# Attention before two expert layers: the multiplication of x and its high part's copy queued behind the score of 128 keys

## The chip, the cores and the metric

The kernel runs on one core of a Trainium2 chip. The metric is the device time of one execution in microseconds; the median of three executions is 2105.64 us. TensorE does the matrix products, VectorE (DVE) and ScalarE (ACT) the elementwise work and the reading of the accumulators, GpSimd (POOL) elementwise work on on-chip data, and SyncE (SP) issues the DMAs.

## The reference, cut to what matters

```python
# attention: q, k, v of (4 batches, 8 heads, 576 positions, 64)
scores = scale * np.matmul(q, k.transpose(0, 1, 3, 2))
scores = np.where(block_i >= block_j, scores, -1e9)      # blocks of 64 positions
scores = scores - np.max(scores, axis=-1, keepdims=True)
attn = np.exp(scores)
attn = attn / (np.sum(attn, axis=-1, keepdims=True) + 1e-09)
x = np.matmul(attn, v)       # then turned to (2304 tokens, 512)
# first layer
h = x @ w_in
x = np.maximum(0.01 * h, h) @ w_out
# second layer: a gate over 8 experts, balanced by 8 rounds of row and column sums
...
for e in range(E):
    out += P[:, e:e + 1] * (np.maximum(x @ w1[e], 0.0) @ w2[e])
```

A query block of 64 positions sees the key blocks up to its own. The x that the attention gives is what the first layer multiplies.

## The kernel before, in words

The attention comes first. Its 32 heads are taken in pairs: NP = 16 pairs, and a pair's two heads share the 128 partitions. Query block i (0 to 8) of a pair needs 64 * (i + 1) keys, so its score is a product of 64, 128, ... 512 columns; the ninth block has 576 keys and is done as two products of 288. Three accumulator banks (tag "sc") go round among the scores, so the score of a block takes the bank that the exponential three scores earlier has read.

For each block `score(p, i)` issues, in this order: the product (line 323, tile `sc`); on VectorE the maximum over the keys, negated (line 324, tile `nmax`); on ScalarE the exponential, with its sum (line 332, tile `ex`). The exponentials are then turned on TensorE 128 columns at a time, four turned tiles to a bank (`turn_attn`, line 363, tile `tr`) and copied out by ScalarE or VectorE (lines 370 and 372, tile `at`). `weigh` multiplies them with the values (lines 385 and 388, tile `av`, one buffer of two banks).

`split_x(p)` ends a pair. On VectorE one multiplication takes the accumulators of the values by the reciprocal sums (line 396, `xs`, in which `by_feature` holds the reciprocals, spread by DMA). On ScalarE a copy rounds the result to the high part of x (line 405, `xhfirst` or `xhlate`), and on GpSimd a subtraction gives the low part (line 406). Where a batch crosses the border between the two x tiles, copy and subtraction are each cut in two.

The work of the pairs is staggered. In pass p of the loop the scores of pair p + 1 are taken in the order 8, 7, 0, 6, 1, 5, 2, 4, 3, and beside each score stands work of other pairs: the queries and keys of pair p + 2 are turned (`turn_q`, `turn_k`, `turn_tail`) and those of pair p + 3 loaded, the exponentials of pair p are turned, and the values of pair p - 1 are weighed and its x split. Beside score 7 stood, before, the turn of the keys, the value products, `split_x` of pair p - 1 and the first turn of pair p:

```python
7: [("fol", turn_k), ("far", load_rows, kraw, k), *values, ("prv", split_x), ("cur", turn_attn, 0)],
...
1: [],
```

TensorE's instructions run in the order of this text (`tc.manual_schedule` names it alone). The order of the other engines is set by a planner, which reorders by its own reckoning of when each instruction's inputs are ready. `tc.issue_after(t)` adds an edge: instructions traced inside the block that run on the engine of `t` are planned behind `t`. It is used for two things before: the steps that split the first layer's weights (two behind score 8, three behind score 7) are queued behind the latest maximum, and the spreading of the sums behind the latest load of values.

The first layer (its products stand at lines 499 and 519) follows directly on TensorE, then the experts, which take most of the span; neither holds a changed line.

Of the kernel before, what the change touches and what calls it, by code (L numbers as in the profile page):

```python
# [27 lines left out]
def f32(ap):  # L28
    return ap.bitcast(F32)
# [7 lines left out]
def block_attention_mlp_moe(  # L37
# [15 lines left out]
    nc = tc.nc  # L53
# [39 lines left out]
    def x_parts(c, t0, t1):  # L93

        if t0 < XCUT:
            return [t[:, c, t0:t1] for t in x_first]
        return [t[:, c, t0 - XCUT:t1 - XCUT] for t in x_late]
# [117 lines left out]
    def attention(att, ps_sc, ps_tr, ps_av):  # L215
        qraw = att.tile([P, NFULL, P], F32, name="qraw")
        kraw = att.tile([P, NFULL, P], F32, name="kraw")
# [93 lines left out]

        latest = [None]

        def score(p, i):
            n = BLK * (i + 1)
            cuts = [(0, n)] if n <= 512 else [(0, n // 2), (n // 2, n)]
            nm, sm = nmax[p % 2], ssum[p % 2]
            part = []  # L320
            for s, (lo, hi) in enumerate(cuts):
                sc = ps_sc.tile([P, 512], F32, name="sc", tag="sc")[:, 0:hi - lo]
                nc.tensor.matmul(sc, qbd[p % 2][:, i, :], kT[p % 2][:, lo:hi], start=True, stop=True)  # L323
                latest[0] = nc.vector.tensor_reduce(  # L324
                    out=nm[:, i + s:i + s + 1], in_=sc, axis=AX.X, op=ALU.max, negate=True
                )
                part.append(sc)
            x = nm[:, i:i + 1]
            if len(cuts) > 1:
                nc.vector.tensor_tensor(out=x, in0=x, in1=nm[:, i + 1:i + 2], op=ALU.min)  # L330
            for s, (lo, hi) in enumerate(cuts):
                nc.scalar.activation(  # L332
                    out=ex[p % 2][:, off[i] + lo:off[i] + hi], in_=part[s], func=AF.Exp,
                    bias=x, scale=1.0, accum_out=sm[:, i + s:i + s + 1],
                )
            if len(cuts) > 1:
                nc.gpsimd.tensor_tensor(
                    out=sm[:, i:i + 1], in0=sm[:, i:i + 1], in1=sm[:, i + 1:i + 2], op=ALU.add
                )
# [51 lines left out]
                )  # L391

        def split_x(p):
            b, hp = divmod(p, NPAIR)
            t = av.pop(p)
            nc.vector.tensor_tensor(  # L396
                out=xs.rearrange("p (i q) -> p i q", q=BLK), in0=t[:, o:o + S].rearrange("p (i q) -> p i q", q=BLK),
                in1=by_feature[p % 2].rearrange("p (q i) -> p i q", i=NQ), op=ALU.mult,
            )
            t0, t1 = b * S, (b + 1) * S  # L400
            cuts = [t0, XCUT, t1] if t0 < XCUT < t1 else [t0, t1]
            for u0, u1 in zip(cuts, cuts[1:]):
                hi, lo = x_parts(hp, u0, u1)
                y = xs[:, u0 - t0:u1 - t0]
                nc.scalar.copy(out=hi, in_=y)
                nc.gpsimd.tensor_tensor(out=lo, in0=y, in1=f32(hi), op=ALU.subtract)

        NP = B * NPAIR
# [4 lines left out]
        values = [("prv", weigh, 0, h, part) for part in range(2) for h in range(2)]  # L413
        values += [("prv", weigh, c, h, 1) for c in range(1, NKC) for h in range(2)]
        beside = {
            8: [("fol", turn_q), ("far", load_rows, qraw, q)],
            7: [("fol", turn_k), ("far", load_rows, kraw, k), *values, ("prv", split_x), ("cur", turn_attn, 0)],
            0: [("cur", turn_attn, 1)],
            6: [("cur", turn_attn, 2), ("nxt", load_v)],
            1: [],  # L420
            5: [("fol", turn_tail), *tails_far],
            2: [("cur", turn_attn, 3)],
            4: [("cur", turn_attn, 4), ("cur", spread_totals)],
# [33 lines left out]
        for p in range(-1, NP + 1):  # L457
            who = {"prv": p - 1, "cur": p, "nxt": p + 1, "fol": p + 2, "far": p + 3}
            if 0 <= p < NP:
                totals(p)  # L460
            for t, i in enumerate(turn_order if p >= 0 else opening):
                if p + 1 < NP:
                    score(p + 1, i)
                for w, f, *a in (beside if p >= 0 else beside_opening)[i]:
                    if 0 <= who[w] < NP:
                        f(who[w], *a)
                for _ in range({0: 2, 1: 3}.get(t, 0) if p >= 0 else 0):
                    if steps:
                        with ExitStack() as queued:
                            if p + 1 < NP:  # L470
                                queued.enter_context(tc.issue_after(getattr(latest[0], "ins", latest[0])))
                            steps.pop(0)()
# [50 lines left out]
    with (  # L523
        tc.tile_pool(name="att", bufs=1) as att,
        tc.tile_pool(name="ps_sc", bufs=3, space=bass.MemoryType.PSUM) as ps_sc,
        tc.tile_pool(name="ps_tr", bufs=3, space=bass.MemoryType.PSUM) as ps_tr,
        tc.tile_pool(name="ps_av", bufs=1, space=bass.MemoryType.PSUM) as ps_av,
    ):
        with tc.manual_schedule(engines={mybir.EngineType.PE}):
            attention(att, ps_sc, ps_tr, ps_av)  # L530
# [345 lines left out]
    for m, (r, b, f, first, last) in enumerate(todo):  # L876
# [11 lines left out]
        if r + 1 == len(runs):  # L888
            k = f - first
# [68 lines left out]
    for n in range(0, NGR, 2):  # L958
        p, e, i = groups[n]
# [74 lines left out]
```

## Time and profile before

| what | value |
|---|---|
| median of three runs | 2105.64 us (2105.45 to 2106.79) |
| the profiled execution's own time | 2106.03 us |
| its span, first to last instruction | 2104.2 us |
| mean granted TensorE clock | 1.000 |
| TensorE busy | 2095.8 us, 10776 matmuls |
| weight loads busy | 1846.2 us |
| VectorE, ScalarE, GpSimd busy | 1428.0, 898.3, 478.3 us |
| last value product of the attention, start | 204.4 us |
| first product of the first layer, start | 204.57 us |

Busy matmul time counts each matmul from its start to a modelled end; matmuls overlap, so the starts of consecutive groups say more than their durations. An instruction's row can likewise reach a little past the start of the next on the same engine. A wait is put down to the instruction that released it, as far as the trace's semaphore events show it.

### The profile page before, as it was taken

The page shows a single profiled execution, that of the slowest core. Times are in us where ns is not written, and L with a number is a line of the kernel's source. Part 1 is how long each engine was busy: PE and PEld are TensorE (multiplying, and loading weights), DVE is VectorE, ACT ScalarE, POOL GpSimd, SP SyncE. Part 2 cuts the span into 40 slices and gives each one's busy share as a digit, 9 for nine tenths or more (in the row PEclk, how much of TensorE's full clock was granted, in tenths as well). Part 3 has the DMA queues.
Part 4 walks back from the last instruction along what each step waited for, and adds up shares of the span by engine and source line. Part 5 has one row for each costly group of instructions (what it writes and reads, how often), then busy time and mean ns, then how long its engine had stood idle before and what let it go on. Part 6 is the DMA issues. An engine that isn't in the chain of part 4 may idle for free.

```text
span 2104.2 us, 28785 instructions
## 1 busy us (share of the span) xinstructions
PE 2095.8 (100%) x10776; PEld 1846.2 (88%) x10776; DVE 1428.0 (68%) x2321; ACT 898.3 (43%) x1859; POOL 478.3 (23%) x526
## 2 busy tenths in 40 slices
PE   9999999999999999999999999999999999999999
PEld 6666898988899899899899889989989988998998
DVE  7786656565468766766777676676678667667665
ACT  7776332222344443443453444344345344434432
POOL 2222212131003212221222221222122122122210
PEclk9999999999999999999999999999999999999999
DMA  5542111010022212212212221221222222122120
GB/s 139 131 121 75 41 40 51 31 56 25 1 61 81 72 49 81 81 41 80 81 60 91 81 71 51 81 81 41 80 81 82 69 80 72 50 81 81 41 81 30
DMA packets 153533, 142.99 MB, mean 68 GB/s; under 512 B 65073, under 2 KB 122417, under 8 KB 153393
## 3 DMA queue, kind: packets, MB, share of 16 engines
q1 hardware_dynamic: 152192, 140.86, 22.5%
q8 instruction: 84, 1.38, 0.3%
q14 instruction: 57, 0.46, 0.1%
q10 hardware_dynamic: 1200, 0.30, 0.1%
HBM read 136.33 MB, written 4.79 MB: 67 GB/s over the span
## 4 chain that ended last, share of the span: by engine, by line
PE 97%; DVE 1%; DMA 0%; ACT 0%; issue 0%; SPq 0%; DVEq 0%; ACTq 0%
PE o L829 37%; PE h_ps L775 33%; PE h_ps L499 9%; PE o L519 9%; PE sc L323 3%; PE av L388 2%; PE tr L363 1%; DVE xs L396 1%; DVE nmax L324 0%; ACT ex L332 0%; DMA qraw<-in_q_dram 0%; DVE at L372 0%; PE qm L297 0%; PE km L303 0%; PE l_ps L633 0%; PE av L385 0%
## 5 line engine op out<-in xcount | busy, mean ns | idle before, releaser
L829 PE MATMUL o<-w2h,xhlate 128*128 128x512 f32 x1152 | 402.6, 390 | 0.0
L829 PE MATMUL o<-w2h,xllate 128*128 128x512 f32 x1152 | 401.6, 389 | 0.0
L783 ACT COPY s<-h_ps 128x384 f32<-128x384 f32 x288 | 138.0, 480 | 555.1 <-PE h_ps L775 555.0
L792 DVE TENSOR_TENSOR c<-h_ps,s 128x384 f32<-128x384 f32 x288 | 155.8, 554 | 313.1 <-PE h_ps L775 303.2
L716 POOL TENSOR_TENSOR wa<-wraw 128x256 f32<-128x256 f32 x96 | 88.0, 917 | 1170.6 <-DVE w1l L734 1144.3
L775 PE MATMUL h_ps<-xhS,w1h 128*128 128x384 f32 x768 | 257.1, 335 | 0.0
L775 PE MATMUL h_ps<-xlS,w1h 128*128 128x384 f32 x768 | 256.5, 334 | 0.0
L775 PE MATMUL h_ps<-xhS,w1l 128*128 128x384 f32 x768 | 256.5, 334 | 0.0
L829 PEld LDWEIGHTS o<-w2h,xllate 128*128 128x128 f32 x1152 | 216.2, 188 | 45.5
L829 PEld LDWEIGHTS o<-w2h,xhlate 128*128 128x128 f32 x1152 | 216.2, 188 | 43.4
L829 PE MATMUL o<-w2l,xhlate 128*128 128x512 f32 x576 | 224.7, 390 | 0.0
L829 PE MATMUL o<-w2l,xllate 128*128 128x512 f32 x576 | 224.4, 390 | 0.0
L842 DVE SCALAR_TENSOR_TENSOR xa<-o,pr,xa 128x512 f32<-128x512 f32 x264 | 189.2, 741 | 50.1 <-PE o L829 50.1
L775 PE MATMUL h_ps<-xhA,w1l 128*128 128x384 f32 x576 | 193.0, 335 | 0.0
L775 PE MATMUL h_ps<-xhA,w1h 128*128 128x384 f32 x576 | 193.0, 335 | 0.0
L775 PE MATMUL h_ps<-xlA,w1h 128*128 128x384 f32 x576 | 192.7, 335 | 0.0
L734 DVE TENSOR_TENSOR w1l<-wraw,w1h 128x512 fp32r<-128x512 f32 x192 | 172.6, 936 | 1.5 <-ACT w1h L733 1.5
L734 DVE TENSOR_TENSOR w1l<-wa,w1h 128x512 fp32r<-128x512 f32 x192 | 160.4, 838 | 0.2 <-ACT w1h L733 0.2
L798 ACT ACTIVATE xllate<-c 128x384 fp32r<-128x384 f32 x144 | 75.7, 526 | 184.1 <-DVE c L792 184.1
L775 PEld LDWEIGHTS h_ps<-xhS,w1h 128*128 128x128 f32 x768 | 144.2, 188 | 0.1
L775 PEld LDWEIGHTS h_ps<-xlS,w1h 128*128 128x128 f32 x768 | 144.2, 188 | 0.0
L775 PEld LDWEIGHTS h_ps<-xhS,w1l 128*128 128x128 f32 x768 | 144.1, 188 | 0.0
(155 smaller groups left out, 3995.6 us busy)
## 6 DMA issues: line engine op xcount, KB each, us to landing
wraw<-in_moe_w_dram SPq DMA_DIRECT2D x192, 512.0 KB, 4.3
wraw<-in_moe_w_in_dram SPq DMA_DIRECT2D x16, 512.0 KB, 3.7
wraw<-in_moe_w_out_dram SPq DMA_DIRECT2D x16, 512.0 KB, 3.6
by_feature<-row SPq DMA_DIRECT2D x32, 144.0 KB, 3.2
out_dram<-xa SPq DMA_DIRECT2D x18, 256.0 KB, 2.0
qraw<-in_q_dram SPq DMA_DIRECT2D x32, 128.0 KB, 2.8
vraw<-in_v_dram SPq DMA_DIRECT2D x32, 128.0 KB, 2.5
kraw<-in_k_dram SPq DMA_DIRECT2D x30, 128.0 KB, 3.2
```

Source lines behind the costliest of these rows:

```text
L323: nc.tensor.matmul(sc, qbd[p % 2][:, i, :], kT[p % 2][:, lo:hi], start=True, stop=True)
L388: nc.tensor.matmul(av[p][r, 512 + P * max(c - 1, 0):512 + S - P], lhsT, a[:, q0:, :], start=c == 0, stop=c == NKC - 1,)
L499: nc.tensor.matmul(ps[:, 0:n], w[:, c, cols], x, start=c == 0 and s == 0, stop=c == KC - 1 and s == 2,)
L519: nc.tensor.matmul(ps[:, 0:n], w[:, cut], h[:, 0:n], start=start and m == 0, stop=stop and m == 2)
L716: nc.gpsimd.tensor_tensor(out=one[:, 0], in0=a21, in1=a22, op=ALU.add)
L734: nc.vector.tensor_tensor(out=lo, in0=x, in1=f32(hi), op=ALU.subtract)
L775: mm = nc.tensor.matmul(ps, w[:, c], x[:, c], start=first and c == 0 and s == 0, stop=c == 1 and s == 2, skip_group_check=True,)
L783: nc.scalar.copy(out=t, in_=bank[n, name][:, 0:HT])
L792: nc.vector.tensor_tensor(out=c, in0=x, in1=part[n, add], op=ALU.add)
L798: nc.scalar.activation(out=hi, in_=x, func=AF.Relu),
L829: mm = nc.tensor.matmul(o, h, w, start=m == 0, stop=m == 11)
L842: nc.vector.scalar_tensor_tensor(out=a, in0=o, scalar=pr[:, tt, e:e + 1], in1=a, op0=ALU.mult, op1=ALU.add)
```

## The change

`split_x` moves from the work beside score 7 to the work beside score 1 (128 keys), three scores later in the text. Its body becomes `multiply_x`, and `split_x` calls it inside a block that plans its VectorE instruction behind the latest maximum and its ScalarE copies behind the latest exponential; in the order of the passes these are the last ones of score 1 of pair p + 1. The edges exist where pair p + 2, counted from the pair that is multiplied, is still to be scored. The work itself is unchanged.

```diff
-        latest = [None]
+        latest, latest_exp = [None], [None]
...
             for s, (lo, hi) in enumerate(cuts):
-                nc.scalar.activation(
+                latest_exp[0] = nc.scalar.activation(
                     out=ex[p % 2][:, off[i] + lo:off[i] + hi], in_=part[s], func=AF.Exp,
...
         def split_x(p):
+            with ExitStack() as queued:
+                if p + 2 < NP:
+                    for t in (latest[0], latest_exp[0]):
+                        queued.enter_context(tc.issue_after(getattr(t, "ins", t)))
+                multiply_x(p)
+
+        def multiply_x(p):
             b, hp = divmod(p, NPAIR)
             t = av.pop(p)
...
-            7: [("fol", turn_k), ("far", load_rows, kraw, k), *values, ("prv", split_x), ("cur", turn_attn, 0)],
+            7: [("fol", turn_k), ("far", load_rows, kraw, k), *values, ("cur", turn_attn, 0)],
...
-            1: [],
+            1: [("prv", split_x)],
```

## Rows read from the trace of the kernel before

**Rows 1.** Busy time by engine in two passes, from value products to value products.
```profile
core 0: us, PE busy (x) PEld busy (x) DVE busy (x) ACT busy (x) POOL busy (x), PEclk, DMA share, GB/s
52.52:64.69 12.17, 12.11 (x79) 8.37 (x78) 9.20 (x22) 9.20 (x29) 4.13 (x5) 1.00 0.55 142
125.55:137.81 12.26, 12.24 (x80) 8.44 (x79) 10.24 (x25) 9.29 (x30) 1.99 (x4) 1.00 0.43 101
```

**Rows 2.** The chain of waits in the pass from 52.9 us: start, us, what.
```profile
55.52 1.20 DVE xs L396
...
58.87 0.59 PE sc L323 x2
```

**Rows 3.** TensorE in order of time in that pass: start us, us, what.
```profile
56.48 0.92 PE L323 MATMUL sc<-kT,qbd 128*128 128x448 f32 x2
...
58.54 0.27 PE L308 MATMUL qk_tail<-ident,tails 128*128 128x128 f32 x1
58.87 0.59 PE L323 MATMUL sc<-kT,qbd 128*128 128x192 f32 x2
...
59.83 0.81 PE L323 MATMUL sc<-kT,qbd 128*128 128x320 f32 x2
60.48 0.60 PE L363 MATMUL tr<-ident,ex 128*128 128x128 f32 x4
60.91 0.60 PE L323 MATMUL sc<-kT,qbd 128*128 128x256 f32 x2
...
61.89 1.14 PE L323 MATMUL sc<-kT,qbd 128*128 128x288 f32 x4
...
63.30 1.02 PE L323 MATMUL sc<-kT,qbd 128*128 128x512 f32 x2
64.16 0.60 PE L303 MATMUL km<-ident,kraw 128*128 128x128 f32 x4
```

**Rows 4.** VectorE in the same pass; in brackets idle time before, and who ended it.
```profile
55.52 1.20 DVE L396 TENSOR_TENSOR xs<-av,by_feature 128x576 f32<-128x576 f32 x1 [1.89 <-PE av L388]
...
56.76 0.69 DVE L372 COPY at<-tr 128x512 f32<-128x512 f32 x1
57.43 0.62 DVE L324 TENSOR_REDUCE nmax<-sc 128x1 f32<-128x448 f32 x1
57.98 0.68 DVE L372 COPY at<-tr 128x512 f32<-128x512 f32 x1
58.57 0.75 DVE L324 TENSOR_REDUCE nmax<-sc 128x1 f32<-128x128 f32 x2
...
60.68 0.49 DVE L324 TENSOR_REDUCE nmax<-sc 128x1 f32<-128x320 f32 x1 [0.82 <-PE sc L323]
...
62.58 0.94 DVE L324 TENSOR_REDUCE nmax<-sc 128x1 f32<-128x288 f32 x2 [0.20 <-PE sc L323]
```

**Rows 5.** ScalarE in the same pass.
```profile
56.75 0.67 ACT L405 CAST xhfirst<-xs 128x576 fp32r<-128x576 f32 x1
...
58.09 0.63 ACT L332 ACTIVATE ex<-sc,nmax 128x448 f32<-128x448 f32 x1 [0.37 <-DVE nmax L324]
...
59.32 0.37 ACT L332 ACTIVATE ex<-sc,nmax 128x128 f32<-128x128 f32 x1
...
59.68 0.57 ACT L332 ACTIVATE ex<-sc,nmax 128x384 f32<-128x384 f32 x1
...
60.63 0.59 ACT L370 COPY at<-tr 128x512 f32<-128x512 f32 x1
61.20 0.53 ACT L332 ACTIVATE ex<-sc,nmax 128x320 f32<-128x320 f32 x1
...
62.04 0.58 ACT L370 COPY at<-tr 128x512 f32<-128x512 f32 x1 [0.22 <-PE tr L363]
62.52 0.48 ACT L332 ACTIVATE ex<-sc,nmax 128x256 f32<-128x256 f32 x1
...
63.50 1.20 ACT L289 ACTIVATE qbd<-qm 64x512 f32<-64x512 f32 x2 [0.41 <-PE qm L297]
```

## Prediction: what the change does to the time

> **What bounds the kernel now.** I read the page first: TensorE is busy for almost the whole span at the full granted clock, and the attention, where alone the changed lines run, takes the first 204.6 us of 2104.2. There the program is a loop over pairs of heads, so I cut it into single passes, from the first value product of one pass to that of the next. A pass lasts 12.17 us (12.26 us in the four passes where the high part's copy is cut in two), and TensorE is busy in 12.11 us of it, VectorE in 9.20 to 10.24, ScalarE in 9.2 [rows 1]. Busy matmuls overlap, so that alone doesn't say that TensorE sets the pass. The chain of waits comes next, and it seems to speak for the change: behind the value products it leaves TensorE, goes through the multiplication of x on VectorE (1.20 us), and comes back to TensorE only with the score of 192 keys at 58.87 [rows 2]. Last I read one pass in order of time, engine by engine, to see whether that detour holds TensorE up.
>
> It doesn't. The 512-key score takes 0.86 us from its start (63.30) to the next start (64.16), that is 1.68 ns for each key; the second 288-key score therefore starts 0.48 us behind the first. VectorE, idle for 0.20 us before, began the first 288-key maximum at 62.58, 0.69 us behind the start of its score (61.89): 0.48 for the columns and 0.21 until the maximum can begin [rows 3, 4]. By the same sum the 448-key score that starts at 56.48 can be taken up at 56.48 + 0.75 + 0.21 = 57.44, and it was at 57.43 [rows 3, 4]. VectorE could have been there only 0.07 us sooner: from a copy of the turned attention to the next maximum it needs 0.59 us (57.98 to 58.57), and there it took 0.67 (56.76 to 57.43) [rows 4]. So the maximum of 448 keys waits for TensorE's own score, not for the multiplication; the two ways tie, and the chain shows one of them. Behind it come the exponential at 58.09, and the score of 192 keys at 58.87, which takes the bank that this exponential frees [rows 3, 5]. That wait stays when the multiplication goes.
>
> **What the change removes.** Both moved instructions sit in idle time now. VectorE waits 1.89 us for the value products before the multiplication [rows 4]; ScalarE is idle for 0.37 us before the exponential of 448 keys even with the copy ahead of it [rows 5]. I put the removal at nothing in the ten passes of the common kind: the cover is the wait for TensorE's 448-key score. In the four longer passes it may give back their difference, 12.26 - 12.17 = 0.09 us each [rows 1], 0.4 us in all. The bounds: nothing below, 0.09 us in all 14 passes (1.3 us) above.
>
> **What it adds.** The code holds the multiplication behind the maximum of 128 keys on VectorE and the copy behind the exponential of 128 keys on ScalarE, in the 14 passes with a next pair to score and a previous one to multiply (p = 1 to 14; the last two passes have no such edge). No instruction and no DMA is added; SP's queue keeps its order. The POOL subtraction follows the copy by its data, about 3 us later; POOL is busy for 4.13 us of such a pass [rows 1], and I put it at nothing. The accumulators that the multiplication reads are next written at the next pass's value products, some 5 us later; nothing too.
>
> What counts is what now queues behind the two. On VectorE the pair of maxima of 128 and 384 keys starts at 58.57 and takes 0.75 us, of which some 0.55 belong to the 384 keys (between 0.49 for 320 and 0.62 for 448), so the one of 128 hands over at about 58.77 [rows 4]. The multiplication then runs until 59.97, and the maximum of 384 keys until 60.52 instead of 59.32. VectorE gets that back soon: it has 0.82 us of idle time before the 320-key maximum and 0.20 before the next [rows 4]. ScalarE doesn't. From 58.09 to 62.52 it stands still only for 0.22 us [rows 5]. The exponential of 128 keys starts at 59.32 and lets the 320-key score go at 59.83, 0.51 us later; the one of 448 keys needs 0.78 (58.09 to 58.87) [rows 3, 5]. In between I take 0.62, 0.67 and 0.73 us for 256, 320 and 384 keys. In the new order the copy starts with the end of the multiplication at 60.00 and ends at 60.67 (its 0.67 us [rows 5]), and the exponential of 384 keys, at 59.68 now, starts there. Then:
> - The score of 256 keys needs the bank of that of 384: 60.67 + 0.73 = 61.40 in place of 60.91 [rows 3], late by 0.49 us.
> - The exponential of 320 keys follows 1.52 us behind that of 384 (59.68 to 61.20) [rows 5]: 62.19, its bank free at 62.86. The second half of the score of 576 keys needs it: 61.89 + 0.49 + 0.48 = 62.86. No further wait.
> - The copy of turned attention at 62.04 follows 0.62 us behind it when its 0.22 us of idle time goes, and the exponential of 256 keys 0.48 us behind that [rows 5]: 63.29, its bank free at 63.91. The score of 512 keys would start at 63.30 + 0.49 = 63.79 [rows 3], and waits until 63.91: late by 0.61 us in all.
>
> Whole durations are a little long: the 0.59 us copy at 60.63 is followed 0.57 us later, the 0.58 us one at 62.04 after 0.48 us [rows 5]. With 0.58 for the copy the delay is 0.52 us. I take 0.55, nearer to the lower end as the rows mostly overlap. The next pass begins with ScalarE's and VectorE's waits for TensorE, so nothing is carried over and nothing won back. Below, the cost is nothing if the planner finds a gap for the copy (third rival); above, it is the order of the first rival.
>
> The sum: 14 passes by 0.55 us is 7.7 us, less 0.4 us, 7.3 us. The profiled execution took 2106.03 us with a span of 2104.2; it would be 2113.3 with 2111.5. It lies 0.4 us above the median of 2105.64, so against the runs it is 2112.9; I say 2113.0.
>
> The Trainium skill, PSUM — Partial Sum Buffer, section Engine vs sequencer instructions, calls the queues of ScalarE and VectorE strict first in, first out. That speaks against this change: a copy that waits for the multiplication holds up the exponential behind it, and by that rule the 7.3 us stand; if later work could pass it, the cost would be near nothing. No row here shows work passing.
>
> **The rivals.**
> - *A worse order on ScalarE.* The planner, not the text, orders VectorE and ScalarE. The copy of turned attention that stands at 60.63 [rows 5] reads transposes that lie between the scores at 58.87 and 59.83 [rows 3], so it becomes ready at about the moment the multiplication ends. If it goes first (60.00 to 60.57), the high part's copy ends at 61.2, and the 256-key score starts at 61.2 + 0.73 = 61.9, late by nearly 1 us: 14 by 0.95, 13.3 us, 2118.5. For it: a near tie. Against it: it stands later in the text.
> - *The gaps take it in part.* If the planner lets the maxima of 384 and 192 keys go first, the multiplication fills the 0.82 us gap [rows 4], the exponential of 384 keys keeps its time, and only the end of ScalarE's run is late: 0.6 us for the copy, less the 0.22 us gap and the 0.16 us by which the bank of the 256-key score (62.52 + 0.62) is free ahead of the score of 512 keys at 63.30 [rows 3, 5], some 0.2 us a pass: 2.8 us, 2108.4. Against it: the multiplication is ready long before that maximum.
> - *No effect.* ScalarE has 0.41 us of idle time before the scaling of the turned queries at 63.50 [rows 5]. A copy planned behind the exponential of 256 keys would cost nothing: 2105.3.
> - *Faster.* The chain of waits is right and the tie is not one. The score of 192 keys starts 0.33 us behind the start of the tail's transpose (58.54), and one transpose takes 0.11 (four in 0.43 from 60.48) [rows 3]: 0.22 us of waiting. It goes when the 448-key maximum starts sooner by that much: 3.1 us in 14 passes, with the 1.3 us above 4.4, so 2101.2. It decides from the point where that maximum starts earlier than 0.95 us behind its score. Against it: the sum that gave 57.44. The Trainium skill, Perfetto Trace Analysis, section Identifying the Most-Contended Engine, measures TensorE by its weight loads, not by its matmuls. The loads take 8.37 of 12.17 us, 69%, less than VectorE's 76% [rows 1]; by that TensorE has room, and this rival would win. The starts of the scores, spaced by their columns, disagree.
>
> **How the numbers follow.** My forecast 0.45, the worse order 0.17, the gaps 0.18, no effect 0.12, faster 0.05; 0.03 are left for a planner that also changes its orders behind the attention. Within 0.2% (4.2 us, about what these runs can tell from no change) lie the gaps and no effect. So faster 0.05, same 0.30, slower 0.65. The likeliest case alone spans 2111.5 to 2115. The range must reach down to no effect and up to the worse order: 2105.0 to 2119.0.
>
> **What would show it.** Right: passes 1 to 14 of about 12.7 us and the last two unchanged; ScalarE's copy to the high part between the exponentials of 128 and 384 keys, with a wait for the multiplication before it; TensorE's 256-key score waiting for an exponential; the 448-key maximum still 0.95 us behind its score; VectorE idle for some 2.6 us ahead of the 64-key maximum; everything behind the attention only shifted. Wrong: the copy elsewhere in ScalarE's order, passes of 12.2 us or less, or a different order of the matmuls behind 205 us.

## The result, and the profile after

| | before | after |
|---|---|---|
| median of four executions | 2105.6 us (2105.45 to 2106.79) | 2119.84 us (2119.23 to 2120.92) |
| ratio of after to before | | 1.0067, 95% interval 1.0049 to 1.0084 |
| the profiled execution: time, span | 2106.03, 2104.2 us | 2119.23, 2117.4 us |
| a pass of the common kind, a long one | 12.17, 12.26 us | 13.13, 13.22 us |
| first value product of the first pass, first product of the first layer | 28.18, 204.57 us | 27.66, 217.67 us |

The kernel became slower, by 14.2 us in the medians and 13.2 us between the two profiled executions. The first layer starts 13.1 us later and the span behind it has not changed (2117.4 - 217.67 = 1899.7 against 2104.2 - 204.57 = 1899.6), so all of it lies ahead of the first layer, in the attention. The 14 passes with the new edges lost 13.6 us together: twelve of them 0.95 to 0.97 us each, and the two last, which are shorter (11.67 and 9.27 us before), 0.97 and 1.15. The first value product came 0.5 us earlier in this execution. The forecast was 2113.0 us with a range up to 2119.0: the sign was right, the forecast loss about half of the measured one, and the time 0.8 us above the range.

The busy time by engine in a pass of each kind, from value products to value products, as in [rows 1]:

```profile
core 0: us, PE busy (x) PEld busy (x) DVE busy (x) ACT busy (x) POOL busy (x), PEclk, DMA share, GB/s
53.92:67.05 13.13, 12.38 (x80) 8.40 (x79) 9.16 (x22) 9.14 (x28) 4.13 (x5) 1.00 0.54 131
132.71:145.92 13.21, 12.38 (x79) 8.39 (x78) 10.17 (x25) 9.23 (x29) 1.98 (x4) 1.00 0.40 91
```

No work was added: VectorE, ScalarE and GpSimd are busy for as long as before, to within 0.1 us. TensorE's busy time rises from 12.11 to 12.38 us with the same matmuls, since a modelled matmul grows where it waits (the score of 256 keys below: 0.70 us in place of 0.60), and for the other 0.75 us of the pass it stands still. Where, its timeline shows (the pass that starts with the value products at 53.92, so 1.40 us later than the one of [rows 3]):

```profile
57.87 0.92 PE L323 MATMUL sc<-kT,qbd 128*128 128x448 f32 x2
...
60.27 0.59 PE L323 MATMUL sc<-kT,qbd 128*128 128x192 f32 x2
...
61.23 0.81 PE L323 MATMUL sc<-kT,qbd 128*128 128x320 f32 x2
61.87 0.60 PE L363 MATMUL tr<-ident,ex 128*128 128x128 f32 x4
63.17 0.70 PE L323 MATMUL sc<-kT,qbd 128*128 128x256 f32 x2 [0.69 <-ACT ex L332]
...
64.25 1.14 PE L323 MATMUL sc<-kT,qbd 128*128 128x288 f32 x4
...
65.66 1.02 PE L323 MATMUL sc<-kT,qbd 128*128 128x512 f32 x2
```

Up to the transposes at 61.87 every start lies exactly 1.40 us behind that of before, or 1.39 (the scores of 448, 192 and 320 keys: 56.48, 58.87, 59.83). The score of 256 keys, due at 60.91 + 1.40 = 62.31, comes at 63.17: 0.86 us late. From there to the next score it takes 1.08 us in place of 0.98, and from there on nothing more is lost (64.25 to 65.66 is 1.41, as 61.89 to 63.30 was). 0.86 + 0.10 is the 0.96 us of the pass.

VectorE in the same pass, and then ScalarE:

```profile
57.63 0.22 DVE L324 TENSOR_REDUCE nmax<-sc 128x1 f32<-128x64 f32 x1 [2.61 <-PE sc L323]
...
58.83 0.62 DVE L324 TENSOR_REDUCE nmax<-sc 128x1 f32<-128x448 f32 x1
...
59.97 0.28 DVE L324 TENSOR_REDUCE nmax<-sc 128x1 f32<-128x128 f32 x1
60.16 1.18 DVE L403 TENSOR_TENSOR xs<-av,by_feature 128x576 f32<-128x576 f32 x1
61.26 0.55 DVE L324 TENSOR_REDUCE nmax<-sc 128x1 f32<-128x384 f32 x1
```

```profile
59.49 0.64 ACT L332 ACTIVATE ex<-sc,nmax 128x448 f32<-128x448 f32 x1 [1.08 <-DVE nmax L324]
...
60.72 0.37 ACT L332 ACTIVATE ex<-sc,nmax 128x128 f32<-128x128 f32 x1
...
61.38 0.67 ACT L412 CAST xhfirst<-xs 128x576 fp32r<-128x576 f32 x1 [0.20 <-DVE xs L403]
61.96 0.58 ACT L370 COPY at<-tr 128x512 f32<-128x512 f32 x1
62.44 0.58 ACT L332 ACTIVATE ex<-sc,nmax 128x384 f32<-128x384 f32 x1
```

Two things are to be seen. The maximum of 448 keys starts 0.96 us behind its score (57.87 to 58.83; before 0.95), with the multiplication no longer ahead of it: nothing was gained there. And ahead of the exponential of 384 keys now stand three things in a row: the wait for the multiplication, the high part's copy, and the copy of a group of turned exponentials, which before stood behind the exponential of 192 keys, at 60.63 [rows 5]. The planner has moved that copy too, ahead of the exponentials of 384 and 192 keys: below, this is called the swap, and that copy the swapped copy. The 256-key score follows 0.73 us behind the start of the exponential of 384 keys.

### The profile page after: what moved, and what is told of

Its sections match the earlier page's. It is cut to its first block, busy times and chain, and to the rows that moved or that the text cites. A ratio compares the mean times of both kernels' runs of the same rounds, so it can differ in the third digit from the quotient of the medians.

```text
span 2117.4 us, 28785 instructions
## 1 busy us (share of the span) xinstructions
PE 2099.0 (99%) x10776; PEld 1846.3 (87%) x10776; DVE 1426.1 (67%) x2321; ACT 897.7 (42%) x1859; POOL 479.2 (23%) x526
## 4 chain that ended last, share of the span: by engine, by line
PE 95%; DVE 2%; ACT 1%; issue 1%; DMA 1%; POOL 0%; SPq 0%; DVEq 0%; POOLq 0%; ACTq 0%
PE o L836 37%; PE h_ps L782 33%; PE h_ps L506 9%; PE o L526 9%; PE sc L323 2%; PE av L388 2%; PE tr L363 1%; DVE xs L403 1%; DVE nmax L324 1%; ACT ex L332 0%; ACT at L370 0%; DMA wraw<-in_moe_w_in_dram 0%; PE l_ps L640 0%; PE qm L297 0%; PE av L385 0%
```

## The experiments

**The theory** behind the first four (A): the score of 256 keys waits for the bank that the exponential of 384 keys reads, and everything that puts this exponential off counts, also the swapped copy. Against it stood B, VectorE's late maximum alone, and C, the swap of the two ScalarE instructions alone. All ratios are to the kernel before, run beside the experiments on the same chip (its medians there: 2105.76 us for experiments 1 to 4, 2106.27 for 5 to 8, and 2105.64 for 9 and 10, which ran on another chip than the rest).

**1. The swapped copy put back behind the exponential of 192 keys** (`t1_turn_behind`), the rest as changed:

```diff
             if g in ((0, 3, 5) if p + 1 < NP else (0, 2, 4, 6)):
-                nc.scalar.copy(out=dst, in_=tr[:, 0:n])
+                with ExitStack() as queued:
+                    if g == 3 and p + 1 < NP:
+                        queued.enter_context(tc.issue_after(getattr(latest_exp[0], "ins", latest_exp[0])))
+                    nc.scalar.copy(out=dst, in_=tr[:, 0:n])
```

> The changed kernel with one more edge: ScalarE's copy of the fourth group of turned exponentials is planned behind the exponential of 192 keys, as it stood before the change. The high part's copy alone then stands between the exponentials of 128 and 384 keys. Theory A (the 256-key score waits for the bank of the exponential of 384 keys, which the multiplication, the high part's copy and the copy of the turned group hold up one after the other): the exponential of 384 keys starts 0.48 us sooner than in the changed kernel, a pass is late by about 0.5 us in place of 0.95, and the kernel takes 2112.6 us (2111.5 to 2113.5). Theory B (VectorE's late maximum of 384 keys alone): no change, 2119.8. Theory C (the swap of the two ScalarE instructions is the whole loss): 2105.6.

Measured: 2112.73 us, ratio 1.0032 (1.0020 to 1.0045); passes of 12.64 us. ScalarE, and the score that waits:

```profile
60.96 0.67 ACT L415 CAST xhfirst<-xs 128x576 fp32r<-128x576 f32 x1 [0.21 <-DVE xs L406]
61.54 0.58 ACT L332 ACTIVATE ex<-sc,nmax 128x384 f32<-128x384 f32 x1
```

```profile
62.26 0.70 PE L323 MATMUL sc<-kT,qbd 128*128 128x256 f32 x2 [0.21 <-ACT ex L332]
```

This is the order that the prediction had summed, and its time is nearly the one forecast (2113.0), in part by luck: a pass lost 0.47 us where 0.55 were summed, and the 0.4 us that were taken off for the long passes did not come. The swap alone is the other half: 13.13 - 12.64 = 0.49 us a pass.

**2. Only the copy moved** (`t2_copy_edge`): the edge for the multiplication left out, so that the planner puts it where it stood before. The diff is against the changed kernel.

```diff
-                    for t in (latest[0], latest_exp[0]):
+                    for t in (latest_exp[0],):
```

> The changed kernel with the edge for ScalarE's copy alone; the multiplication is planned as early as before the change. Theory A: the copy adds 0.58 us ahead of the exponential of 384 keys; its bank comes free 0.08 us late, and the run of exponentials ends 0.2 us late: 14 passes by 0.2, less 0.4 us: 2108.0 us (2106.5 to 2109.5). Theory B: 2105.6. Theory C: 2105.6.

Measured: 2108.22 us, ratio 1.0011 (1.0002 to 1.0020); passes of 12.33 us, 0.16 above those of before. The time is the one expected, but in other pieces: the 256-key score comes 0.05 us late, its follower 0.11 more, the score of 512 keys does not wait, and the long passes (12.42 us) gave nothing back. ScalarE and TensorE:

```profile
60.49 0.58 ACT L332 ACTIVATE ex<-sc,nmax 128x384 f32<-128x384 f32 x1
```

```profile
61.21 0.70 PE L323 MATMUL sc<-kT,qbd 128*128 128x256 f32 x2
```

**3. The multiplication moved, the copy out of the way** (`t3_mult_alone`): `split_x` cut into its two halves, the copy with the subtraction moved to the end of the run of exponentials, the swapped copy held as in the first experiment.

```diff
-            1: [("prv", split_x)],
+            1: [("prv", mult_x)],
...
-            3: [("cur", turn_attn, 5), ("cur", turn_attn, 6)],
+            3: [("cur", turn_attn, 5), ("cur", turn_attn, 6), ("prv", copy_x)],
```

> The multiplication behind the maximum of 128 keys as in the changed kernel; the high part's copy goes behind the exponential of 256 keys, and the copy of the turned group stays behind the exponential of 192 keys. So ScalarE's order up to there has nothing added, and VectorE's is that of the change. Theory A: the exponential of 384 keys starts with the end of its maximum, some 0.75 us late; its bank is late by 0.26 us, the end of the run by 0.38: 14 by 0.38 is 5.3, 2110.5 us (2109 to 2112). Theory B: 2119.8. Theory C: 2105.6.

Measured: 2111.21 us, ratio 1.0025 (1.0015 to 1.0035); passes of 12.54 us, the long ones now too. ScalarE stands still before the exponential of 384 keys, until VectorE has its maximum; the copy of the turned group, whose transposes stand at 61.97, keeps its place behind:

```profile
63.13 0.58 ACT L332 ACTIVATE ex<-sc,nmax 128x384 f32<-128x384 f32 x1 [0.67 <-DVE nmax L324]
...
64.10 0.58 ACT L373 COPY at<-tr 128x512 f32<-128x512 f32 x1
```

```profile
61.97 0.60 PE L363 MATMUL tr<-ident,ex 128*128 128x128 f32 x4
...
63.85 0.70 PE L323 MATMUL sc<-kT,qbd 128*128 128x256 f32 x2
```

**4. Multiplication early, copy at the end of the run** (`t4_copy_late`): the second experiment with `split_x` beside score 3, which makes the edge one to the exponential of 256 keys.

```diff
-            1: [("prv", split_x)],
+            1: [],
...
-            3: [("cur", turn_attn, 5), ("cur", turn_attn, 6)],
+            3: [("cur", turn_attn, 5), ("cur", turn_attn, 6), ("prv", split_x)],
```

> The multiplication as early as before the change, the high part's copy behind the exponential of 256 keys, in ScalarE's 0.41 us of idle time. The copy no longer precedes the exponential of 64 keys, which makes the four long passes 0.09 us shorter. Theory A: 2105.2 us (2104.5 to 2106). Theory B and C: 2105.6. If the chain of waits through the multiplication counted before the change, nothing moves here either, since the multiplication stays.

Measured: 2107.42 us, ratio 1.0009 (1.0001 to 1.0018): 1.7 us more than before, where no loss was expected. The score of 256 keys no longer waits, and most passes last 12.17 us, two of the four long ones too; but two last 12.84 and 12.92, and three 12.28 to 12.36. GpSimd's and VectorE's timelines ahead of the first of these, from its value products at 88.56 on:

```profile
87.90 1.41 POOL L413 TENSOR_TENSOR xlfirst<-xs,xhfirst 128x576 fp32r<-128x576 f32 x1
```

```profile
87.99 1.34 DVE L330 TENSOR_TENSOR nmax<-nmax 128x1 f32<-128x1 f32 x1
...
92.44 1.20 DVE L403 TENSOR_TENSOR xs<-av,by_feature 128x576 f32<-128x576 f32 x1
...
94.29 0.62 DVE L324 TENSOR_REDUCE nmax<-sc 128x1 f32<-128x448 f32 x1
```

The minimum of the two halves of the ninth block, one column, takes 1.34 us in place of 0.10, and ends with GpSimd's subtraction, which the late copy has moved beside it. VectorE's weight steps then run late, the multiplication starts 3.9 us behind the value products in place of 3.0, and the maximum of 448 keys starts 1.8 us behind its score: here the multiplication holds up TensorE. A held minimum alone does not do it. It takes 1.27 us ahead of passes of 12.17 us too, where at most three weight steps follow and VectorE catches up before the multiplication. Ahead of the pass of 12.92 us, a second instruction is held: a weight step, 0.71 us in the kernel before, beside a GpSimd subtraction of weights of 1.27 us:

```profile
116.10 1.52 DVE L182 SCALAR_TENSOR_TENSOR wraw<-wraw,wb 128x512 f32<-128x512 uint32 x1
```

**What the four say together.** From the start of the exponential of 384 keys to that of the score of 256 keys it takes 0.73 us in the changed kernel and 0.72 in the first three experiments (61.54 to 62.26 and 63.13 to 63.85 in two of them), while in the fourth the exponential starts early and the score comes 1.23 us behind it, as before (59.68 to 60.91). The distance between TensorE's scores of 320 and 256 keys is 1.08 us before, and 1.13, 1.34, 1.46 and 1.94 in these four kernels, while that from the exponential stays. The score's delay is that exponential's. B and C each fail on the first three.

**5 and 6. Four banks for the scores, two for the transposes**, with the kernel before (`t5_before_four`) and with the changed one (`t6_after_four`):

```diff
-        tc.tile_pool(name="ps_sc", bufs=3, space=bass.MemoryType.PSUM) as ps_sc,
-        tc.tile_pool(name="ps_tr", bufs=3, space=bass.MemoryType.PSUM) as ps_tr,
+        tc.tile_pool(name="ps_sc", bufs=4, space=bass.MemoryType.PSUM) as ps_sc,
+        tc.tile_pool(name="ps_tr", bufs=2, space=bass.MemoryType.PSUM) as ps_tr,
```

> The kernel before with four accumulator banks for the scores and two for the transposes, in place of three and three. Theory A (scores wait for the bank of the exponential three scores back): the waits of the scores of 192 and 320 keys, 0.22 and 0.09 us a pass, go; passes of some 11.85 us, 15 of them: 2101.0 us (2099.5 to 2103). Theory D (TensorE's own stream sets the pass, the gaps are not waits for a bank): 2105.6.

> The changed kernel with four banks for the scores and two for the transposes. The score of 256 keys then takes the bank of the 128-key exponential, which stands ahead of the moved copy. Theory A: most of the 14 us of the change go, 2103 us (2101 to 2107), within 0.3% of the kernel before with the same banks. Theory E (ScalarE or VectorE as a whole is too late, whatever bank a score takes): the distance between the two stays 14 us, 2115.

Measured: 2101.40 us for the kernel before with these banks, ratio 0.9975 (0.9966 to 0.9985), passes of 11.78 us: the waits of the scores of 192 and 320 keys were waits for a bank. The 192-key score now follows 0.11 us behind the tail's transpose, in place of 0.33 [rows 3]:

```profile
59.06 0.27 PE L308 MATMUL qk_tail<-ident,tails 128*128 128x128 f32 x1
59.17 0.49 PE L323 MATMUL sc<-kT,qbd 128*128 128x192 f32 x2
```

This version is faster than both kernels. The changed kernel with these banks missed its expectation: 2114.67 us, ratio 1.0039 (1.0025 to 1.0053), 13.3 us behind its counterpart, so the distance stayed. That is the figure of theory E; but no score waits there any more, and the loss is again a wait for one bank. TensorE's wait has gone to the transposes behind the score of 320 keys, and VectorE's timeline shows for what:

```profile
87.08 0.70 PE L323 MATMUL sc<-kT,qbd 128*128 128x320 f32 x2
88.62 0.63 PE L363 MATMUL tr<-ident,ex 128*128 128x128 f32 x4 [0.84 <-DVE kT L292]
```

```profile
86.43 1.18 DVE L403 TENSOR_TENSOR xs<-av,by_feature 128x576 f32<-128x576 f32 x1
87.53 0.81 DVE L324 TENSOR_REDUCE nmax<-sc 128x1 f32<-128x384 f32 x2
88.26 0.21 DVE L292 COPY kT<-qk_tail 128x64 f32<-128x64 f32 x1
```

With two banks these transposes need the one of the tail, and the tail's copy stands behind the multiplication and two maxima.

**7. The multiplication narrowed in the kernel before** (`t7_narrow`), to ask whether its early place cost anything. The kernel leaves out the multiplication of eight of the nine query blocks:

```diff
+        nc.gpsimd.memset(xs, 0.0)
...
             nc.vector.tensor_tensor(
-                out=xs.rearrange("p (i q) -> p i q", q=BLK), in0=t[:, o:o + S].rearrange("p (i q) -> p i q", q=BLK),
-                in1=by_feature[p % 2].rearrange("p (q i) -> p i q", i=NQ), op=ALU.mult,
+                out=xs[:, 0:BLK], in0=t[:, o:o + BLK], in1=by_feature[p % 2][:, 0:BLK], op=ALU.mult,
             )
```

> The kernel before with the multiplication on 64 columns in place of 576; the other columns of its result are zeros, set once at the start. VectorE is free about 1 us sooner for the maxima behind it. Theory A (the maximum of 448 keys waits for TensorE's own score, so the early multiplication is covered): passes of 12.17 us, the four long ones too, 2105.2 us (2104.6 to 2106). Theory F (the chain of waits is right, the multiplication holds up the scores): 0.2 to 0.3 us a pass less, 2101 to 2102.5.

Measured: 2105.78 us against 2106.27, ratio 0.9997 (0.9988 to 1.0006); passes of 12.17 us, the long ones too. TensorE and VectorE:

```profile
56.37 0.92 PE L323 MATMUL sc<-kT,qbd 128*128 128x448 f32 x2
```

```profile
55.41 0.22 DVE L396 TENSOR_TENSOR xs<-av,by_feature 128x64 f32<-128x64 f32 x1 [1.89 <-PE av L388]
...
57.33 0.62 DVE L324 TENSOR_REDUCE nmax<-sc 128x1 f32<-128x448 f32 x1
```

With the multiplication 1 us shorter the maximum of 448 keys still starts 0.96 us behind its score, and the time is the same within the interval. F falls.

**8. GpSimd's subtraction in pieces** (`t8_pieces`), in the kernel of experiment 4:

```diff
-                nc.gpsimd.tensor_tensor(out=lo, in0=y, in1=f32(hi), op=ALU.subtract)
+                for g in range(0, u1 - u0, 192):
+                    cut = slice(g, min(g + 192, u1 - u0))
+                    nc.gpsimd.tensor_tensor(out=lo[:, cut], in0=y[:, cut], in1=f32(hi)[:, cut], op=ALU.subtract)
```

> The kernel with the copy behind the exponential of 256 keys, and GpSimd's subtraction cut into pieces of at most 192 columns. Theory G (the one-column minimum on VectorE, which took 1.27 us in place of 0.10 while the subtraction ran, waits for the GpSimd instruction under way): it takes 0.6 us or less, the passes of 12.8 us go, and the kernel takes 2105.4 us (2104.8 to 2106.5). Otherwise, where the loss has another cause: 2107.4.

Measured: 2107.10 us against 2106.27, ratio 1.0003 (0.9994 to 1.0012). The held minimum takes 0.42 to 0.45 us, where it took up to 1.34, and the passes of 12.8 us are gone; single ones of 12.42 and 12.34 remain. In the pass of 12.42 us the weight step at line 182 is still held (1.48 us), beside a GpSimd subtraction that was not cut. The wait of the minimum is shown; the time missed the range of theory G and lies between the two expectations, and whether it differs from that of experiment 4 the intervals don't say.

**9 and 10. The halves of the change with four and two banks**: the second experiment (`t9_copy_four`) and the third (`t10_mult_four`) with the banks of experiments 5 and 6, and no other edit.

> Four banks for the scores and two for the transposes, with ScalarE's copy of the high part behind the exponential of 128 keys and the multiplication as early as before the change. Theory H (what the moved copy cost with three banks, 0.16 us a pass, was the wait for the bank of the exponential of 384 keys; with four banks no score takes that bank so soon): passes of 11.8 us as in the kernel before with four banks, 2101.4 us (2100 to 2103). Theory E (ScalarE as a whole is too late): 0.2 us a pass more, 2104.5.

> Four banks for the scores and two for the transposes, the multiplication behind the maximum of 128 keys, the copy of the high part at the end of ScalarE's run. Theory H: VectorE alone makes the whole loss with these banks, since the key tail's copy stands behind the multiplication and two maxima, and the transposes that need its bank wait 0.8 us: passes of 12.8 us, 2114.5 us (2113 to 2117). Theory E, with ScalarE as the cause: the 0.67 us of the copy are gone from its run, passes of 12.2 us or less, 2106.

Measured: 2108.34 us for the copy alone, ratio 1.0013 (1.0004 to 1.0022), passes of 12.33 us, and 2117.94 us for the multiplication alone, ratio 1.0058 (1.0045 to 1.0070), passes of 12.94 us. The first lies above what either theory gave: 0.55 us a pass more than the 11.78 of experiment 5. The wait is again one for a bank of the transposes, here for ScalarE's copy of the turned group, which the planner puts behind the moved copy and the exponential of 384 keys:

```profile
76.07 0.76 PE L363 MATMUL tr<-ident,ex 128*128 128x128 f32 x5 [0.46 <-ACT at L370]
```

```profile
74.30 0.66 ACT L412 CAST xhfirst<-xs 128x576 fp32r<-128x576 f32 x1
74.86 0.58 ACT L332 ACTIVATE ex<-sc,nmax 128x384 f32<-128x384 f32 x1
75.43 0.58 ACT L370 COPY at<-tr 128x512 f32<-128x512 f32 x1
```

In the second the transposes behind the 320-key score wait 0.84 us for the tail's copy, as H said; its time is 0.9 us above the range given. No run had more banks in both rings at once, so it is not shown whether the loss would then go.

## Why the prediction was right or wrong

- *What bounds a pass.* Right. TensorE's stream sets it, with waits for banks that experiment 5 found worth 0.39 us a pass, and the early multiplication was covered by the wait for the 448-key score: the changed kernel and the narrowed multiplication both leave that maximum 0.96 us behind its score. The chain of waits in [rows 2] named a path that was only as long as another (0.08 us apart by the rows that the prediction reads, not 0.07).
- *The sign and the place.* Right. The score of 256 keys waits for the bank of the exponential of 384 keys, in all 14 passes, and the last passes and all behind the attention are as before.
- *The copy's place.* The step that failed is the sentence that the copy ends at 60.67 and "the exponential of 384 keys, at 59.68 now, starts there". The planner put the copy of the turned group in between, at a price of 0.49 us a pass. In the pass of [rows 5] that exponential would stand at 61.04 (62.44 - 1.40) and the 256-key score at 61.77 in place of 61.40. The sum took ScalarE's order of before as given, with the one copy put in. With the turned group's copy put back, the kernel takes 2112.73 us.
- *The first rival* had this instruction, the cost of a pass (0.95 us; measured 0.96) and nearly the time (2118.5), but in the other order, turned group first, and 0.17 of the chance. On the chip the high part's copy went first and the turned group's second, ahead of an exponential that was late itself: its maximum ended at 61.81, ScalarE was free of the high part's copy at 61.96. I had weighed the turned group only against the high part's copy, not against the exponential, which the multiplication makes late on VectorE. Why the planner ranks the two so is not shown; that it does is in the rows of ScalarE. The measured time lies above this rival's, and above the range whose upper end it set, in part since the 0.4 us that it too took off for the long passes did not come and the last of the 14 passes lost 1.15 us; the prediction had taken all 14 for full ones.
- *The sizes in the order that I summed* came out in other pieces (first experiment): the 256-key score is late by 0.38 us, not 0.49, since the copy hands over after 0.58 us; 0.09 more follow behind a score that has waited; and the later wait of 0.12 us for the 512-key score did not come. 0.47 in all, against 0.52 to 0.61.
- *The four long passes* gave nothing back: 13.22 - 13.13 = 0.09 us, as before. The copy in two pieces costs that at its new place too. Where the copy leaves the run they shrink to the common length: all four in experiment 3, two of the four in experiment 4.
- *The parts don't add up as they stand.* Copy alone 0.16 us a pass, multiplication alone 0.37, both 0.47, with the swap 0.96: the two moves overlap a little, and the swap comes on top.
- *The strict queues* (the Trainium skill, PSUM — Partial Sum Buffer, section Engine vs sequencer instructions): the traces agree. In the changed kernel ScalarE waits 0.20 us for the multiplication at 61.38; the exponential behind it was not ready by then, so this alone would not tell. In experiment 3 ScalarE stood still for 0.67 us until 63.13, and the copy of the turned group, whose transposes stand at 61.97 with the next score behind them at 62.51, did not pass: it ran at 64.10.

## What to carry to other kernels

A path in the chain of waits is worth removing only if it is longer than the next one: sum the other way to the same instruction (here the score's own columns and 0.21 us) before believing it. An instruction moved out of an idle slot to where its engine feeds a ring of buffers without slack costs part of its length (here 0.16 us a pass for a copy of 0.67, 0.37 for a multiplication of 1.2), and an edge that fixes two instructions lets a planner rearrange a third, so read the planned order of the neighbours too. Banks given to one ring are taken from another: the kernel before gained 0.39 us a pass by it, while in the changed kernel the waits moved to the other ring and the distance between the two stayed.

## What the runs showed of the hardware that was not expected

A VectorE instruction of one column with both operands in SBUF can be held for the whole of a GpSimd instruction: the minimum at line 330 took 0.10 us (median) before, 1.24 to 1.34 us beside the subtraction of 576 columns in experiments 3 and 4 (1.41 us by itself), 0.83 to 0.84 beside the subtraction in two pieces of the long passes, and 0.42 to 0.45 with pieces of 192 columns. A weight step with two inputs in SBUF took 1.52 us in place of 0.71 beside a GpSimd subtraction of weights; no run varied that one. The Trainium skill, SBUF — State Buffer, section SBUF: two separate sides, says that VectorE and GpSimd share one pair of ports as an exclusive lock, held for a whole instruction, and that a VectorE instruction with two SBUF inputs competes for it; the trace agrees, and the time that the loser waits follows the length of the other's instruction. In the kernel before, the subtraction ran while VectorE read from accumulators, and the minimum never met it.

Banks came back at a constant pace: 0.71 to 0.73 us from the start of the 384-key exponential to the start of the score that takes its bank, in four kernels in which that score waits. The figure alone proves no wait: in experiment 5, where the score takes another bank, the same distance is 0.70 to 0.72 us by TensorE's own order.
